# Block-sparse attention with a gated convolution: low words of w_out and of the taps in PSUM, ten more zero products, another order of all pieces

## The chip, the cores and the metric

The kernel runs on one core of one Trainium2 chip. The metric is device time in microseconds of one execution. The core's engines are named as in the profile: PE is TensorE, DVE VectorE, ACT ScalarE, POOL GpSimd, and SP the engine from whose queue every DMA is issued. Each engine works through its own list of instructions in order and waits where an instruction needs another engine's result.

## The reference

Four sequences of 768 positions, eight heads of 64. Each query sees the 31 keys around it and 24 summaries of blocks of 32 (maximum of the keys, mean of the values). The heads' outputs side by side are `x` (4 x 768 x 512), which goes through a causal convolution of five taps, a sigmoid gate and two 512 x 512 products:

```python
k_sum = k.reshape(B, H, nb, block, D).max(axis=3)
v_sum = v.reshape(B, H, nb, block, D).mean(axis=3)
scores_l = np.where(mask_l, scale * q @ k.T, -1e9)
scores_s = scale * q @ k_sum.T + np.log(block)
a = softmax(np.concatenate([scores_l, scores_s], axis=-1))
x = a @ np.concatenate([v, v_sum], axis=2)
gate_pre = sum(conv_w[k] * xp[:, k:k + S, :] for k in range(5))
out = (1 / (1 + np.exp(-gate_pre)) * (x @ w_val)) @ w_out
```

## The kernel before, in words

The work is cut into 24 units `u` (sequence, third of 256 positions, half of the heads) and 12 groups `g` (sequence, third; two units each). Everything is fp32. A product at full precision for the late groups is made of three cheaper ones: each factor is split into a rounded head (`xh`, `gh`, slot 0 of `wsplit`) and the rest (`xl`, `gl`, slot 1).

For a unit, `mm_s` puts the scores of two tiles into PSUM on TensorE (L558), `snorm` adds the mask and finds the minimum of the negated scores on VectorE (L573), `exps` is ScalarE's exponential (L586), `row_sum` and `recip` give 1/sum (VectorE), `norm` scales the rows (GpSimd, L600), `tp` transposes on TensorE (L610), `pcopy` brings the result to SBUF, `mm_x` multiplies by the values (L621, or L639 and L641 in the first and last units). `x_full`, `x_add`, `x_head` and `x_rest` make `xf`, `xh`, `xl`. `ginit` and `tap` (four per unit and half, VectorE, L677) are the convolution, `gate` a tanh. For a group, `val_mm` (L705) multiplies by `w_val`, `gated` (VectorE, L713) applies the gate, `out_mm` (L745) multiplies by `w_out`, and `out_scale` and `out_store` send the result away. Group 0 uses the unsplit weights `wf` in both products.

The weights arrive as 8-byte words. The high word of each is turned into a partial float by `rebias` on ScalarE (`sc`, L387). `low_bits` on VectorE shifts the low word right by 29 (L392), and `join` on VectorE puts both together (L396). `w_val` and `w_out` come in four pieces each (`wv0` to `wv3`, `wo0` to `wo3`, 128 x 512), the convolution's taps in one of 128 x 20 (`cw`, result `cwt`). In the kernel before, `low_bits` writes to the place in SBUF where the joined weight will stand, and `join` reads it there. `sc` of `w_val` lies in PSUM, that of the others in SBUF. PSUM has the pool `ps_p` with three banks, used by `val`, `out`, two small transposes and `sc` of `w_val`.

Nothing is scheduled by rules: `ORDER` (L54 to L138) is a list of 1265 words, one for each piece of work, and each engine receives the instructions of its pieces in that order. `W0` to `W23` (`warm_mm`, L335) are products of a tile of zeros, bf16, 512 columns, whose result nobody reads. In the word `ks0.1` the piece is `key_max` of sequence 0 and pair of heads 1 (VectorE, L258), `kc` copies its result into the key tile (GpSimd), `s0.0` is `mm_s` of unit 0, first half, `n0.1.0` `snorm` of unit 0, `Lk`, `Lq`, `Lv`, `Lu`, `Lwo` are loads of keys, queries, values, transposed values and raw weights, `F` fills the sums of the values into a loaded value tile (L369), `O` stores a result (L766), `rb`, `sh` and `or` with a weight's name are `rebias`, `low_bits` and `join`; `rbc`, `shc`, `orc` the same for the taps.

```python
    def join(dst, sc):
        d = dst.bitcast(U32)
        nc.vector.scalar_tensor_tensor(
            d, sc.bitcast(U32), 3, d, ALU.logical_shift_left, ALU.bitwise_or
        )
```

Of the kernel before, what the change touches and what calls it, by code (L numbers as in the profile page):

```python
# [60 lines left out]
m1.0 vt2.2 vc3.1 vc3.0 vt2.3 vt2.4 vc2.0 vc2.1 W23 s3.1 s3.0 t1.1 e2.0.1 e2.1.1 vbc0 rbwv0 shwv2
cd0.1 shwv0 n3.0.0 rr2 n3.0.1 orc rv2 n3.1.0 e3.0.0 c1.1 orwv0 orwv2 rbwv1 shwv1 orwv1 n3.1.1
x0.1 x0.0 t1.0 vb1 Lk1.0 Y0 I0.0 T0.0.0 T0.0.1 ks1.0 wcpwv0 m2.0 m2.1 wcpwv2 wlwv0 wlwv2 Lwv3
Lv1 v0.0.0.0 s4.1 s4.0 c1.0 vbc1 e3.1.1 I0.1 e3.0.1 e3.1.0 rbwv3 n4.0.1 n4.1.1 T0.0.2 n4.1.0
n4.0.0 v0.1.1.0 v0.0.1.0 t2.0 t2.1 c2.0 e4.0.1 c2.1 T0.0.3 rr3 rv3 T0.1.0 T0.1.1 T0.1.2 T0.1.3
e4.0.0 e4.1.0 Lu1.2 Lk1.1 Lq3 Lk1.3 F1 Lk1.2 s5.0 s5.1 x1.0 x1.1 n5.1.0 shwv3 n5.0.0 orwv3
n5.0.1 ks1.1 n5.1.1 G0 Y1 m3.1 kc1.0 m3.0 tv1.2 kc1.1 wcwv1 I1.0 v0.1.0.0 t3.0 I1.1 e4.1.1
T1.1.0 rr4 T1.0.0 rv4 T1.0.1 v0.1.1.1 v0.1.0.1 t3.1 c3.0 wcwv3 c3.1 s6.0 s6.1 x2.1 x3.0 x2.0
x3.1 v0.0.0.1 v0.0.1.1 Lv2 Lu1.1 Lwo0 Lq4 Lwo1 Lu1.0 F2 Lwo2 Lwo3 ks1.3 T1.1.1 n6.1.0 n6.0.1
T1.0.2 n6.0.0 ks1.2 T1.0.3 n6.1.1 T1.1.2 gf0.0 T1.1.3 wlwv1 wlwv3 m4.0 kc1.3 hal1 m4.1 kc1.2  # L70
e5.0.1 e5.1.1 X2 Y2 Y3 X3 Z2 Z3 e5.1.0 e5.0.0 e6.0.0 t4.0 t4.1 G1 I2.1 s7.0 s7.1 n7.0.0 n7.1.1
rr5 n7.0.1 n7.1.0 I2.0 T2.0.0 T2.1.0 rv5 T2.0.1 shwo0 T2.1.1 gf0.1 c4.0 e6.1.0 e7.0.1 e6.1.1
rbwo0 c4.1 e6.0.1 rbwo1 T2.1.2 T2.0.2 orwo0 T2.1.3 shwo1 rr6 T2.0.3 orwo1 shwo2 hal2 tv1.1 m5.0
m5.1 tv1.0 v1.1.0 v1.0.0 v1.0.1 v1.1.1 Lu1.3 Lu2.0 s8.1 x4.0 s8.0 x4.1 e7.0.0 Y4 rbwo2 rv6 G2
Ya4 orwo2 m6.0 o0.0.0 o0.0.1 t5.0 rbwo3 c5.0 I3.0 I3.1 shwo3 n8.1.1 orwo3 t5.1 o0.0.2 t6.0
o0.0.3 gf1.0 T3.1.0 n8.0.0 T3.0.0 tv1.3 c5.1 c6.0 e7.1.0 ob0.0 e7.1.1 Xp4 m6.1 Z4 wcpwo0 T3.1.1
n8.0.1 T3.0.1 rr7 T3.0.2 n8.1.0 T3.0.3 T3.1.2 rv7 T3.1.3 o0.1.0 o0.1.1 o0.1.2 vsp1 x5.1 x5.0
s9.0 s9.1 e8.0.1 e8.0.0 vsc1 tv2.0 wcpwo1 Y5 m7.0 Lv3 Ya5 Lk2.1 Lq5 Lu2.1 O0.0 Lk2.0 F3 Lq6
# [802 lines left out]
```

## Time and profile before

| what | us |
|---|---|
| three runs, median (lowest to highest) | 236.69 (235.08 to 236.76) |
| the profiled execution: its own time | 237.33 |
| its span, first to last instruction | 235.2 |
| TensorE busy | 224.5 |
| VectorE busy | 202.3 |
| GpSimd busy | 173.5 |
| ScalarE busy | 165.3 |

The span is what the trace shows; 2.13 us of the profiled execution's own time lie around it. This execution is 0.64 us above the median. Matmuls are recorded with modelled ends, and the products of scores, values and unsplit weights are recorded twice, so that 8 of them stand as x16.

### The profile page before, as it was taken

Reading aid. Unit: us, or ns where it says so; the run is one execution under the profiler, and the core shown is the slowest. Engines: PE = TensorE matmul, PEld = TensorE weight load, DVE = VectorE, ACT = ScalarE, POOL = GpSimd, SP = SyncE. Lnnn points to the kernel's source line nnn. Section 1 sums busy time; section 2 is a strip of 40 time slices with the busy share of each in tenths; the row PEclk is TensorE's granted clock in tenths of the full one; section 3 lists DMA queues with packets and bytes.
Section 4 is the critical chain, followed back from the end, with each engine's and each line's share of the span. In section 5 each row is a group of like instructions: output and inputs, shape, how many; then the busy total and the mean of one; then the engine's idle time right before and its main releaser. Section 6 shows DMA issues by size and latency. Waiting matters only on the chain.

```text
span 235.2 us, 8434 instructions
## 1 busy us (share of the span) xinstructions
PE 224.5 (95%) x3200; PEld 191.8 (82%) x3200; DVE 202.3 (86%) x740; ACT 165.3 (70%) x562; POOL 173.5 (74%) x262
## 2 busy tenths in 40 slices
PE   7688899998999999999999999999999999999994
...
PEclk9979999999999999999999999999999999999999
...
GB/s 252 403 415 414 413 229 345 308 207 285 332 183 352 124 337 101 292 366 150 243 100 11 0 280 216 91 303 237 96 11 0 25 262 109 47 3 92 0 88 135
DMA packets 16167, 46.20 MB, mean 196 GB/s; under 512 B 2272, under 2 KB 2528, under 8 KB 16128
## 3 DMA queue, kind: packets, MB, share of 16 engines
...
## 4 chain that ended last, share of the span: by engine, by line
PE 64%; DVE 18%; DMA 7%; ACT 5%; issue 2%; SPq 2%; POOL 1%; DVEq 0%; ACTq 0%; POOLq 0%
PE out L745 22%; PE val L705 20%; PE s L558 7%; PE pt L610 6%; PE x L621 6%; DVE g L677 5%; DMA v<-in_vw_dram 4%; DVE sn L573 4%; DVE wf L396 3%; ACT p L586 3%; DMA k<-in_kq_dram 2%; PE x L639 2%; DVE ks L258 1%; DVE wf L392 1%; DMA v<-vs 1%
## 5 line engine op out<-in xcount | busy, mean ns | idle before, releaser
L677 DVE SCALAR_TENSOR_TENSOR g<-xf,cwt,g 128x256 f32<-128x256 f32 x192 | 93.2, 486 | 7.1 <-ACT g L219 3.3
L586 ACT ACTIVATE p<-sn,nm 128x120 f32<-128x120 f32 x192 | 73.5, 387 | 12.5 <-DVE nm L573 10.5
L600 POOL TENSOR_TENSOR p<-p,ri 128x480 f32<-128x480 f32 x48 | 47.5, 1001 | 17.3 <-DVE ri L596 10.5
L705 PE MATMUL val<-xh,wv 128*128 128x256 f32 x352 | 50.0, 285 | 0.1
L573 DVE CUSTOM_DVE_ANT_0 sn<-s,mask 128x120 f32<-128x120 f32 x192 | 44.0, 275 | 3.6 <-PE s L558 3.0
L705 PEld LDWEIGHTS val<-xh,wv 128*128 128x128 f32 x352 | 44.2, 189 | 1.6 <-issue 0.6
L745 PE MATMUL out<-wo,gh 128*128 128x512 f32 (+1 forms) x184 | 45.4, 389 | 0.0
L745 PEld LDWEIGHTS out<-wo,gh 128*128 128x128 f32 x184 | 32.4, 188 | 6.6 <-issue 0.5
L586 ACT ACTIVATION_READ_ACCUMULATOR p<-sn,nm 128x1 f32 x192 | 36.7, 191 | 0.0
L613 ACT COPY pts<-pt 120x512 f32<-120x512 f32 x44 | 24.8, 583 | 15.7 <-PE pt L610 15.7
L721 POOL TENSOR_TENSOR gl<-gf,gh 128x512 fp32r<-128x512 f32 x22 | 28.3, 1293 | 8.6 <-ACT gh L718 8.3
L661 POOL TENSOR_TENSOR xl<-xf,xh 128x512 fp32r<-128x512 f32 x22 | 28.7, 1311 | 6.6 <-DVE xf L652 5.0
L286 POOL TENSOR_TENSOR vT<-vT 128x384 f32<-128x384 f32 (+3 forms) x44 | 25.5, 580 | 3.7 <-DMA vT<-in_vT_dram 1.1
L705 PE MATMUL val<-xl,wv 128*128 128x256 f32 x176 | 27.6, 279 | 0.0
L610 PE MATMUL pt<-ident,p 128*120 128x128 f32 x192 | 26.8, 276 | 0.1
L610 PEld LDWEIGHTS pt<-ident,p 128*120 128x120 f32 x192 | 22.3, 138 | 4.2 <-issue 1.7
L558 PE MATMUL s<-k,q 64*64 64x120 f32 x704 | 24.5, 270 | 0.6 <-DVE ri L596 0.6
L684 ACT ACTIVATE gt<-g 128x512 f32<-128x512 f32 x24 | 14.3, 596 | 14.8 <-DVE g L677 14.8
L745 PE MATMUL out<-wo,gl 128*128 128x512 f32 (+1 forms) x92 | 23.8, 381 | 0.0
L705 PEld LDWEIGHTS val<-xl,wv 128*128 128x128 f32 x176 | 23.6, 189 | 0.0
L558 PEld LDWEIGHTS s<-k,q 64*64 64x64 f32 x704 | 18.5, 135 | 4.8 <-issue 3.0
L745 PEld LDWEIGHTS out<-wo,gl 128*128 128x128 f32 x92 | 16.9, 188 | 3.4
...
## 6 DMA issues: line engine op xcount, KB each, us to landing
...
```

The lines of the kernel that those rows point to most:

```text
L286: nc.gpsimd.tensor_tensor(dst, src[:, :, :n], src[:, :, n : 2 * n], ALU.add)
L558: nc.tensor.matmul(sp(u)[64 * e : 64 * e + 64, h, c * KW : c * KW + KW], qs[64 * h : 64 * h + 64, i * QT : i * QT + QT], ktile[b, pr][64 * ...
L573: nc.vector.tensor_tensor_reduce(sn(u)[:, n, :], sp(u)[:, h, c * KW : c * KW + KW], mask[:, mv, :], -1.0 / math.sqrt(D), 3.0e38, ALU.add, ...
L586: nc.scalar.activation(pr_(u)[:, n, :], sn(u)[:, n, :], AF.Exp, bias=nm(u)[:, n : n + 1], scale=-1.0, accum_out=rs(u)[:, n, 0:1],)
L600: nc.gpsimd.tensor_tensor(pr_(u)[:, w], pr_(u)[:, w], st["ri", u][:, w].unsqueeze(2).broadcast_to([P, TPU, KW]), ALU.mult,)
L610: nc.tensor.transpose(pt[:KW, i, :], pr_(u)[:, TPU * r + i, :], ident)
L613: (eng or nc.scalar.copy)(pts(u)[:, TPU * r : TPU * r + TPU], st.pop(("pt", u, r))[:KW])
L661: nc.gpsimd.tensor_tensor(xl(g)[:, two(hp), :], xf(g)[:, two(hp), HALO:], xh(g)[:, two(hp), :].bitcast(F32), ALU.subtract,)
L677: nc.vector.scalar_tensor_tensor(gp(u)[:, r], xf(g)[:, pr, o : o + SG], cwt[:, pr, o : o + 1], gp(u)[:, r], ALU.mult, ALU.add,)
L705: nc.tensor.matmul(pp[:, r], w, x, start=first and n == 0, stop=last and n == len(terms) - 1)
L721: nc.gpsimd.tensor_tensor(gl(g)[:, two(cp), :], grp["gf", g, cp], gh(g)[:, two(cp), :].bitcast(F32), ALU.subtract)
L745: nc.tensor.matmul(pp, x, w, start=start and n == 0, stop=stop and n == len(terms) - 1)
```

## The change

`low_bits` of the four pieces of `w_out` and of the taps now writes to a tile of its own from `ps_p` in PSUM (`low_put`), and `join` reads the low word there. For `w_val` nothing is changed in this. `ORDER` has ten more zero products, `W24` to `W33`, all its other words stand in another order, and 55 of them name another engine for a copy, a scaling or a cast. Of the list only the beginning and one line are shown.

```diff
--- before.py
+++ after.py
@@ -52,89 +52,89 @@
-ez wz W0 W1 W2 W3 W4 Mi Mu W5 W6 W7 W8 W9 cv Lk0.0 Mm ks0.0 kc0.0 s0.0 W10 Lk0.1 Lk0.2 ks0.1
...
+ez wz W0 W1 W2 W3 W4 W5 Mu Lk0.0 Lk0.1 Mm ks0.0 ks0.1 kc0.0 W6 W7 W8 W9 W10 W11 W12 W13 W14 W15
+W16 W17 W18 W19 W20 W21 s0.0 W22 W23 W24 Lk0.3 Lk0.2 Lc Lwv0 Ln1 Ln0 Ln2 Lq1 Lwv1 Lv0 Lwv2 Ln3
...
@@ -391,15 +391,20 @@
         low = raw.rearrange("p (n two) -> p two n", two=2)[:, 0]
         eng.tensor_scalar(dst.bitcast(U32), low, 29, None, ALU.logical_shift_right)
 
-    def join(dst, sc):
-        d = dst.bitcast(U32)
+    def low_put(nm, n, raw):
+        t = ps_p.tile([P, DM], F32, tag="pp", name=f"low_{nm}")
+        lows[nm] = t[:, :n]
+        low_bits(nc.vector, lows[nm], raw)
+
+    def join(dst, sc, low):
         nc.vector.scalar_tensor_tensor(
-            d, sc.bitcast(U32), 3, d, ALU.logical_shift_left, ALU.bitwise_or
+            dst.bitcast(U32), sc.bitcast(U32), 3, low.bitcast(U32), ALU.logical_shift_left, ALU.bitwise_or
         )
 
     wide = wv.dtype != F32
     wraw = {}
     scaled = {}
+    lows = {}
     wf = cpool.tile([P, 4, DM], F32, tag="wf", name="wf")
 
     def load_w(nm, k):
@@ -416,12 +421,15 @@
 
     def w_low(nm, k):
         if wide:
-            low_bits(nc.vector, wf[:, k], wraw[nm, k])
+            if nm == "wo":
+                low_put(f"wo{k}", DM, wraw[nm, k])
+            else:
+                low_bits(nc.vector, wf[:, k], wraw[nm, k])
 
     def w_join(nm, k):
         raw = wraw.pop((nm, k))
         if wide:
-            join(wf[:, k], scaled.pop((nm, k)))
+            join(wf[:, k], scaled.pop((nm, k)), lows.pop(f"{nm}{k}", wf[:, k]))
         else:
             nc.vector.tensor_copy(wf[:, k], raw.bitcast(F32))
 
@@ -449,11 +457,11 @@
 
     def cw_low():
         if wide:
-            low_bits(nc.vector, cflat, wraw["cw"])
+            low_put("cw", NPR * NK, wraw["cw"])
 
     def cw_join():
         if wide:
-            join(cflat, scaled.pop("cw"))
+            join(cflat, scaled.pop("cw"), lows.pop("cw"))
 
     units = [(b, th, hp) for b in range(B) for th in range(NTH) for hp in range(NHP)]
     NG = B * NTH
```

On VectorE at the start of the program, while the first three units' scores are worked on (`sn_2` is unit 2, `cwt` the taps, `ks_0_2` the key maxima of sequence 0 and pair 2, `ri_0` the row sums of unit 0, `vpad` sums of values), before and then now:

```order
L613 COPY pts_0_313<-pt_0_0_269 120x512
L573 ISA sn_2_315,nm_2_316<-s_2_275,mask_99 128x120
L573 ISA nm_2_316 128x1
L573 ISA sn_2_315,nm_2_316<-s_2_275,mask_99 128x120
L573 ISA nm_2_316 128x1
L392 TENSOR_SCALAR cwt_101<-cwraw_197 128x20
```

```order
L392 TENSOR_SCALAR low_cw_251<-cwraw_177 128x20
L258 TENSOR_REDUCE ks_0_2_253<-k_0_2_175 128x24
L581 ISA sn_1_255,nm_1_256<-s_1_242,mask_99 128x120
L581 ISA nm_1_256 128x1
L581 ISA sn_1_255,nm_1_256<-s_1_242,mask_99 128x120
L581 ISA nm_1_256 128x1
L601 TENSOR_REDUCE ri_0_259<-rs0_109 128x8
L392 TENSOR_SCALAR wf_108<-raw_wv0_179 128x512
L604 RECIPROCAL ri_0_259<-ri_0_259 128x8
L309 TENSOR_REDUCE vpad_103<-vT_0_1_181 128x12
```

The shift of the taps' low words has moved from the middle of unit 2's scores to a place between units 0 and 1, and writes `low_cw` instead of `cwt`.

On VectorE where `w_out` is joined, some 50 us into the program (`g_2` is the convolution of unit 2, `xf_2` the attention's output of group 2, `gf_1_0` the gated product of group 1), with the waits of each instruction, before and then now:

```order
L392 TENSOR_SCALAR wf_108<-raw_wo0_745 128x512 [waits DMAHW0_49]
L677 SCALAR_TENSOR_TENSOR g_2_823<-xf_1_787,cwt_101,g_2_823 128x256 [waits DVE_49]
L713 SCALAR_TENSOR_TENSOR gf_0_1_861<-gt_0_638,val_0_1_527 128x512
L677 SCALAR_TENSOR_TENSOR g_2_823<-xf_1_787,cwt_101,g_2_823 128x256 [waits DVE_49] x2
L396 SCALAR_TENSOR_TENSOR wf_108<-sc_wo0_872,wf_108 128x512 [waits Activation_49]
L677 SCALAR_TENSOR_TENSOR g_2_823<-xf_1_787,cwt_101,g_2_823 128x256 [waits DVE_49]
L392 TENSOR_SCALAR wf_108<-raw_wo1_749 128x512 [waits DMAHW2_49]
L593 TENSOR_REDUCE ri_6_884<-rs2_111 128x8 [waits Activation_49]
L677 SCALAR_TENSOR_TENSOR g_2_823<-xf_1_787,cwt_101,g_2_823 128x256 [waits DVE_49]
L396 SCALAR_TENSOR_TENSOR wf_108<-sc_wo1_877,wf_108 128x512 [waits DVE_49,Activation_49]
L392 TENSOR_SCALAR wf_108<-raw_wo2_757 128x512 [waits DMAHW0_49]
L596 RECIPROCAL ri_6_884<-ri_6_884 128x8 [waits DVE_49]
L657 TENSOR_TENSOR xf_2_889<-xf_2_889,x_4_1_971 128x2x256 [waits PE_49,Activation_49]
L396 SCALAR_TENSOR_TENSOR wf_108<-sc_wo2_1013,wf_108 128x512 [waits DVE_49,Activation_49]
```

```order
L392 TENSOR_SCALAR low_wo0_930<-raw_wo0_726 128x512 [waits DMAHW0_49]
L685 SCALAR_TENSOR_TENSOR g_2_842<-xf_1_661,cwt_101,g_2_842 128x256 [waits DVE_49]
L400 SCALAR_TENSOR_TENSOR wf_108<-sc_wo0_862,low_wo0_930 128x512 [waits DVE_49,Activation_49]
L685 SCALAR_TENSOR_TENSOR g_2_842<-xf_1_661,cwt_101,g_2_842 128x256 [waits DVE_49]
L392 TENSOR_SCALAR low_wo2_994<-raw_wo2_728 128x512 [waits DMAHW1_49,DVE_49]
L685 SCALAR_TENSOR_TENSOR g_2_842<-xf_1_661,cwt_101,g_2_842 128x256 [waits DVE_49]
L400 SCALAR_TENSOR_TENSOR wf_108<-sc_wo2_969,low_wo2_994 128x512 [waits DVE_49,Activation_49]
L685 SCALAR_TENSOR_TENSOR g_2_842<-xf_1_661,cwt_101,g_2_842 128x256 [waits DVE_49]
L665 TENSOR_TENSOR xf_2_973<-xf_2_973,x_4_1_938 128x2x256 [waits PE_49,Activation_49]
L721 SCALAR_TENSOR_TENSOR gf_1_0_1016<-gt_1_1013,val_1_0_882 128x512 [waits Activation_49]
L392 TENSOR_SCALAR low_wo3_1043<-raw_wo3_1023 128x512 [waits DMAHW0_49,DVE_49]
L400 SCALAR_TENSOR_TENSOR wf_108<-sc_wo3_1039,low_wo3_1043 128x512 [waits DVE_49,Activation_49,Pool_49]
```

The shifts write `low_wo` tiles instead of `wf`, a shift and its join stand closer together, piece 1 comes earlier than the part shown, and the shifts of pieces 2 and 3 wait for VectorE's own earlier work.

In SP's queue of DMAs, where the values of group 8 are loaded and filled (`v_8`, and its four fills from `vs_2`), before and then now:

```order
L369 DMA v_6_2180<-vs_2_2101 12x2x512 x4
L249 DMA v_7_2274<-in_vw_dram 128x1024 x2
L369 DMA v_7_2274<-vs_2_2101 12x2x512 x4
L766 DMA out_0_dram<-ob_4_0_2593 128x512
L242 DMA vT_3_2_2596<-in_vT_dram 128x768
L230 DMA q_10_2598<-in_qT_dram 128x1024
L242 DMA vT_3_0_2600<-in_vT_dram 128x768
L249 DMA v_8_2636<-in_vw_dram 128x1024 x2
L766 DMA out_0_dram<-ob_3_1_2323 128x512
L369 DMA v_8_2636<-vs_2_2101 12x2x512 x4
```

```order
L369 DMA v_6_1910<-vs_2_2136 12x2x512 x4
L249 DMA v_7_2201<-in_vw_dram 128x1024 x2
L242 DMA vT_3_3_2342<-in_vT_dram 128x768
L774 DMA out_0_dram<-ob_1_0_1486 128x512
L369 DMA v_7_2201<-vs_2_2136 12x2x512 x4
L249 DMA v_8_2550<-in_vw_dram 128x1024 x2
L242 DMA vT_3_0_2553<-in_vT_dram 128x768
L774 DMA out_0_dram<-ob_4_0_2641 128x512
L230 DMA q_10_2646<-in_qT_dram 128x1024
L369 DMA v_8_2550<-vs_2_2136 12x2x512 x4
```

The load of `v_8` has moved ahead of a load of transposed values, a store and a load of queries, and one load of transposed values stands between it and the fills where there was a store.

## Rows read from the trace of the kernel before

**Rows 1.** The page: busy time by engine; TensorE's busy tenths and clock in 40 slices
```profile
PE 224.5 (95%) x3200; PEld 191.8 (82%) x3200; DVE 202.3 (86%) x740; ACT 165.3 (70%) x562; POOL 173.5 (74%) x262
...
PE   7688899998999999999999999999999999999994
...
PEclk9979999999999999999999999999999999999999
```

**Rows 2.** Busy time in stretches: from:to, length, busy us (xinstructions) by engine, PEclk, DMA
```profile
0.00:10.00 10.00, 7.45 (x49) 2.76 (x49) 5.64 (x19) 2.74 (x9) 3.51 (x19) 1.00 0.82 313
...
10.00:20.00 10.00, 7.20 (x96) 4.93 (x100) 9.08 (x53) 8.08 (x39) 6.77 (x17) 0.83 1.03 413
...
30.00:40.00 10.00, 10.00 (x217) 8.86 (x215) 9.86 (x44) 9.60 (x35) 8.65 (x14) 1.00 0.81 263
...
50.00:60.00 10.00, 9.10 (x121) 5.21 (x114) 10.00 (x25) 8.40 (x25) 9.07 (x12) 1.00 0.65 234
...
150.00:160.00 10.00, 9.60 (x163) 8.78 (x161) 9.17 (x32) 5.49 (x19) 9.75 (x12) 1.00 0.86 270
...
230.00:236.00 6.00, 2.10 (x18) 1.89 (x16) 0.00 (x0) 0.77 (x2) 0.00 (x0) 0.90 0.24 88
```

**Rows 3.** The chain that ended last: start us, us, what ran
```profile
57.26 3.70 PE out L745 x8
...
137.57 9.61 DMA v<-in_vw_dram
...
221.06 11.05 PE out L745 x60
...
232.13 0.38 ACT ob L219
```

**Rows 4.** Timeline of TensorE (PE) and its weight loads (PEld), first 20 us
```profile
1.52 4.45 PE L335 MATMUL warm_out<-warm 128*128 128x512 bf16 x10 [1.52 <-POOL warm L330]
...
4.91 0.15 PEld L335 LDWEIGHTS <-warm 128*128 128x128 bf16 x1 [0.28 <-issue]
...
6.22 0.64 PE L558 MATMUL s<-k 64*64 64x120 f32 x16 [0.25 <-POOL k L272]
...
13.14 1.08 PE L558 MATMUL s<-k 64*64 64x120 f32 x16 [1.13 <-POOL k L272]
```

**Rows 5.** Timeline of VectorE (DVE), first 20 us; idle time and its releaser in brackets
```profile
8.22 0.28 DVE L573 CUSTOM_DVE_ANT_0 sn<-s,mask 128x120 f32<-128x120 f32 x1 [1.27 <-PE s L558]
...
11.87 0.17 DVE L593 TENSOR_REDUCE ri<-rs 128x8 f32<-128x16 f32 x1 [0.22 <-ACT p L586]
...
14.28 0.28 DVE L573 CUSTOM_DVE_ANT_0 sn<-s,mask 128x120 f32<-128x120 f32 x1 [0.31 <-PE s L558]
...
17.05 0.28 DVE L573 CUSTOM_DVE_ANT_0 sn<-s,mask 128x120 f32<-128x120 f32 x1 [0.36 <-PE s L558]
```

**Rows 6.** Lines 396 and 392: count, duration ns min/median/max, first and last start
```profile
L396 DVE SCALAR_TENSOR_TENSOR wf<-sc_wv,wf x4: 673/680/691, 23.2 to 34.0; 128x512 uint32<-128x512 uint32 x4
L396 DVE SCALAR_TENSOR_TENSOR wf<-sc_wo,wf x4: 759/1134/1491, 49.5 to 56.1; 128x512 uint32<-128x512 uint32 x4
L396 DVE SCALAR_TENSOR_TENSOR cwt<-sc_cw,cwt x1: 960/960/960, 21.8 to 21.8; 128x20 uint32<-128x20 uint32 x1
...
L392 DVE TENSOR_SCALAR wf<-raw_wo x4: 419/435/826, 47.3 to 55.0; 128x512 uint32<-128x512 uint32 x4
L392 DVE TENSOR_SCALAR cwt<-cwraw x1: 756/756/756, 17.5 to 17.5; 128x20 uint32<-128x20 uint32 x1
```

**Rows 7.** Timeline of GpSimd (POOL), 53 to 66 us
```profile
54.46 1.07 POOL L648 CAST xh<-xf 128x512 fp32r<-128x512 f32 x1
...
64.13 0.61 POOL L648 CAST xh<-xf 128x512 fp32r<-128x512 f32 x1
```

**Rows 8.** Timeline of TensorE, 52 to 61 us
```profile
52.97 1.13 PE L745 MATMUL out<-wf,gf 128*128 128x512 f32 x2 [0.17 <-ACT sc_wo L387]
...
57.26 3.70 PE L745 MATMUL out<-wf,gf 128*128 128x512 f32 x8 [0.57 <-DVE wf L396]
```

More of the change, by code (lines that the diff above doesn't have):

```diff
@@ L61 @@
[L61 to L78, printed above, removed]
@@ new lines @@
+T0.1.0 rv2 T0.1.1 ks1.0 e3.0.0 e3.1.0 I0.0 e3.1.1 e3.0.1 c1.1 vt3.0 vt3.1 vt3.2 vt3.3 vt3.4
+vc3.0 vt2.3 vt2.4 vc2.1 m2.1 vc3.1 vc2.0 m2.0 kc1.0 Lq2 s4.1 s4.0 Lwv3 Lv1 Lk1.2 Lk1.1 T0.1.2
+n4.0.0 n4.1.0 n4.0.1 T0.0.0 n4.1.1 T0.0.1 shwv3 rr3 v0.0.1.0 v0.1.1.0 vb1 t2.1 e4.1.0 vbc1 s5.1
+s5.0 T0.1.3 rv3 n5.1.0 T0.0.2 n5.0.0 T0.0.3 e4.0.0 e4.1.1 c2.1 rbwv3 x1.0 x1.1 Lk1.3 G0 Y1
+wcpwv2 I1.1 n5.1.1 orwv3 ks1.2 T1.1.0 n5.0.1 ks1.1 v0.0.0.0 t2.0 c2.0 e4.0.1 m3.1 wcpwv1 m3.0
+wlwv1 wlwv2 kc1.1 hal1 wcpwv3 wlwv3 kc1.2 v0.1.1.1 I1.0 v0.1.0.1 v0.0.1.1 t3.1 t3.0 e5.0.0
@@ new lines @@
+T6.0.1 T6.1.3 T6.0.2 rv9 ks2.2 x8.0 s12.0 Y8 e11.1.0 m9.0 hal4 m9.1 Z6 kc2.2 n12.0.0 T6.0.3 G6
+Ya8 I7.0 ob2.1 I7.1 rr10 ks2.3 n12.1.0 n12.0.1 n12.1.1 T7.1.0 T7.0.0 rv10 rr11 T7.0.1 T7.1.1
+T7.1.2 rv11 T7.1.3 o2.0 t9.0 t9.1 c9.1 c9.0 v3.1.1 kc2.3 x9.1 s13.0 s13.1 x9.0 e12.1.1 Lv5 Lq7
+Lu2.1 Lk3.1 Lk3.3 F5 e12.0.0 e12.1.0 Y9 tv2.1 v3.1.0 v3.0.0 n13.1.1 T7.0.2 T7.0.3 G7 I8.1 I8.0
+n13.0.0 n13.0.1 Ya9 n13.1.0 m10.1 m10.0 X9 m11.1 Lu2.2 tv2.2 Xp8 Z8 Z9 t10.1 t10.0 v3.0.1
+e12.0.1 c10.1 e13.1.1 gf3.1 T8.0.0 cd10.0 T8.0.1 rr12 T8.1.0 rv12 T8.0.2 T8.0.3 T8.1.1 T8.1.2
```

133 lines of the change are left out of this document (69 added, 64 removed).

## The prediction

> **What bounds the kernel now.** I read the page first, then the busy time in stretches, the chain that ended last, and the timelines of the places that these point to. On the page TensorE is busy 224.5 of 235.2 us, and its row of tenths is full from the sixth slice to the last but one [rows 1]. The stretches say it more sharply (the engines stand in the order PE, PEld, DVE, ACT, POOL): TensorE is busy 7.45 and 7.20 us of the first two tens, all 10.00 in 30 to 40, 9.10 in 50 to 60, 9.60 in 150 to 160, and 2.10 of the last six [rows 2]. The chain ends with 11.05 us of TensorE's products and a 0.38 us copy from 232.13 on [rows 3]. So the end is set by the start-up, in which TensorE has little to do, then by TensorE's own work, with idle time of 0.9 and 0.4 us in two of the later stretches, and by a tail of about 3 us (2.10 of 6 busy, then copy and store). Products are neither removed nor made shorter. The change can only move the start-up, these small gaps, and make new ones.
>
> The start-up is VectorE's. Its first score piece begins at 8.22, after 1.27 us of waiting for scores, and three short waits follow (0.22, 0.31, 0.36 us) [rows 5]; over 10 to 20 it is busy 9.08, over 50 to 60 all 10.00 [rows 2]. The last two of the three waits are for score products that ran slowly: 16 records took 0.64 us at 6.22 and 1.08 us at 13.14 [rows 4], in the stretch whose granted clock is 0.83, so partly at 1.2 GHz and not at 2.4 [rows 2].
>
> **The change, part by part.** I add up against the profiled execution's own 237.33 us, which lies 0.64 above the median of the three runs, and take that off at the end.
>
> *Zero products ahead of the first scores.* Before, ten stand there and take 4.45 us from 1.52 on; the weights of the tenth are loaded at 4.91 [rows 4], so they follow each other at (4.91 - 1.52) / 8 = 0.42 us, which is the lower clock, since the scores behind them already ran at the short time. Now 22 stand ahead of `s0.0` (the list's first words in the diff). If the clock rises when it did, the first ten end near 5.9 and the twelve others take half as long each, 12 x 0.21 = 2.5 us: `s0.0` starts near 8.4 and ends 0.64 later, and VectorE's first score piece starts near 9.1 instead of 8.22. Before, it began with the second half of the scores, now with the first, so not the whole shift of 2.2 us arrives. Cost +0.9 us on VectorE, bounds 0 and +3.9 (a rival below). The other twelve zero products (34 in all, 22 ahead) stand in TensorE's waits for the next scores; I take them at nothing, and 0.2 us each where such a wait is gone.
>
> *The three short waits.* The next scores now come when VectorE still has key maxima, the taps' shift and a piece of `w_val` to do. I take all 0.9 us as gone, bounds 0 and -0.9.
>
> *The taps.* Their shift took 0.756 us and their join 0.960 for 20 columns, while a join of 512 columns of `w_val` took 0.680 [rows 6]. So it isn't the columns that cost: another small piece on this engine takes 0.17 [rows 5]. What sets the two apart from `w_val`'s join is that both their tensors lie in SBUF, with GpSimd at work beside them. With the low word in PSUM I take 0.2 us each: -1.3 us, bounds 0 and -1.4. Both stand on the path, as VectorE is the engine that the start-up waits for.
>
> *The clock in the start-up.* Zero products keep TensorE at work until near 11 us. Then, as before, it waits for VectorE piece by piece, and the clock may fall again, now between 14 and 22 us, where five groups of 16 score records and the first values' product stand. Each group then costs 0.44 more (1.08 - 0.64), 2.2 us in all, part of it beside VectorE's other work. I take +0.7, bounds 0 and +2.2. The start-up sums to +0.9 - 0.9 - 1.3 + 0.7 = -0.6.
>
> *The four pieces of `w_out`.* Their joins took 1.134 us in the median, up to 1.491, against 0.680 for those of `w_val`, whose high part lies in PSUM [rows 6]. With one tensor in PSUM I take 0.68: 4 x 0.45 = 1.8 us less on VectorE. GpSimd gains too: a cast took 1.07 us beside these joins and 0.61 at 64 us [rows 7]. But only what TensorE waited is on the path: it was idle 0.9 us in this stretch [rows 2], of which the rows name 0.17 for ScalarE's part of `w_out` and 0.57 for the last join [rows 8]. I take -0.9, bounds -1.2 and +0.9. The upper end is the added wait: a low word needs one of three banks, and of `wo3` it holds the one that the second output tile of group 0 needs. Behind that tile's first product stand the rest of group 0's output, the values of unit 5 and the scores of unit 9. The product that follows needs `wo3`'s join in any case, so late joining costs one product here, no more than 1.13 us for two records [rows 8].
> The row has the shift of `w_out`'s low words at 0.435 us, and I leave it at that. The Trainium skill (VectorE: DVE Perf Modes, "Why PSUM operands drop a tier") says that an fp32 operand in PSUM holds an instruction to one element per cycle. An estimate from that page's 0.96 GHz is 512 / 0.96 = 0.53 us, so 0.4 us more for four; by it this part would be -0.5 and the forecast 0.4 later. No row here has a shift into PSUM.
>
> *The new order from 60 us on.* The load of group 8's values took 9.61 us from 137.57 [rows 3], and TensorE lost 0.4 us in 150 to 160, after it. SP's queue now has that load ahead of a store, of queries and of transposed values, so it should land earlier; I take half, -0.2. What new gaps the order makes can't be read from rows of the old one: I take 0, bounds -0.4 and +2.5 (as much as the whole start-up lost in its first ten us, 10.00 - 7.45). The tail keeps its pieces: last product of half a tile, copy, store.
>
> Sum: -0.6 - 0.9 - 0.2 = -1.7. 237.33 - 1.7 = 235.6, less 0.64 is **235.0 us**.
>
> **The rivals.**
> *More is gained.* The clock holds through the start-up (+0.7 falls away), and GpSimd's saved time lets scales and casts come earlier, so that both later gaps vanish (-0.2 - 0.3). For it: more zero products exactly where the clock fell, and the slow casts of rows 7. Against it: zero products end near 11 us, and the slow stretch of before began at 13. Time 235.0 - 1.2 = 233.8, or less.
> *The order pays it back.* TensorE is full from 30 us on, so each piece that is late by more than its slack shows, and 1275 words in a new order have many chances. For it: VectorE is busy 86%, and gaps of 0.9 and 0.4 exist even now. Against it: TensorE's row of tenths shows no slice below 8 after the first third of the program, except the last [rows 1]. With +1.9 of new gaps: 236.9.
> *Slower: the zero products overrun.* They stand in TensorE's queue ahead of the first scores, and if they all run at the lower clock, 22 end at 1.6 + 22 x 0.42 = 10.9, the first scores at 12.0 instead of 6.9; VectorE starts 3.9 late, and the next nine products cost 0.21 more each, 1.9. With the taps and `w_out` still gained: 237.33 + 3.9 + 1.9 - 1.3 - 0.9 - 0.64 = 240.3. For it: the first ten all ran slowly. Against it: the scores right behind them did not. It decides from the eighth product on that runs slowly after the tenth (8 x 0.21 = 1.7 eats the forecast).
>
> **How the numbers follow.** Forecast 0.50, more gained 0.20, paid back 0.20, overrun 0.10. About 1% (2.4 us) is what a measurement of this kernel can tell from no change. Faster by more than that is below 234.3: the second case and a fifth of the forecast's, 0.30. Slower is above 239.1: the overrun, and a fifth of the paid-back case, 0.14. Within, 0.56. The range leaves out most of the overrun, and the outer part of the second case: 232.6 to 239.0. Below, the sum of all lower bounds (-1.4 - 0.9 at the start, -1.2, -0.4) is -3.9, so 232.8; above, the forecast with the bound of +2.5 for new gaps and the clock's full cost is 235.0 + 2.5 + 1.5 = 239.0.
>
> **What would show it right or wrong.** Right: VectorE's first score piece near 9.1 us; the taps' two pieces near 0.2 us; the joins of `w_out` near 0.68 and TensorE's busy time in 50 to 60 near 10; TensorE full from about 28 us; the last product about 1.7 us before 232.1. Wrong in the start: zero products still 0.42 us apart after the tenth, or granted clock below 0.83 in 10 to 20 and low in 20 to 30. Wrong in the rest: stretches after 60 us in which TensorE's busy time is below 9.6, and a chain that there runs through VectorE, GpSimd or a load of values.

## The result, and the profile after

The changed kernel took 233.86 us in the median of six executions (233.49 to 234.50), the kernel before 236.72 (235.08 to 237.78) in six beside it: ratio 0.9887, 95% interval 0.9851 to 0.9923. That is 2.9 us faster, where the forecast of 235.0 expected 1.7. It lies in the range, and at the time of the case "more is gained" (233.8). How large the gain is depends on the executions of before that it is set against, since these are a mixture (shown further below): in a later series, in which that kernel's median was 235.57, the changed kernel was 1.8 us faster (233.78), at a ratio of 0.9908. The profiled execution took 233.49, its span is 231.7 us.

The page of the changed kernel, against [rows 1]: the same engines, VectorE 2.6 us less busy, TensorE's tenths full from the fifth slice to the last but one, and no slice of its clock below 9.

```profile
PE 224.4 (97%) x3210; PEld 191.9 (83%) x3210; DVE 199.7 (86%) x743; ACT 165.4 (71%) x564; POOL 169.0 (73%) x257
...
PE   7988999999999999999999999999999999999994
...
PEclk9999999999999999999999999999999999999999
```

Busy time in stretches, in the columns of [rows 2]:

```profile
0.00:10.00 10.00, 8.37 (x46) 3.33 (x47) 4.22 (x18) 2.02 (x5) 2.64 (x18) 1.00 0.80 298
10.00:20.00 10.00, 8.29 (x131) 5.11 (x135) 9.99 (x56) 9.60 (x44) 8.12 (x17) 1.00 1.03 414
50.00:60.00 10.00, 10.00 (x147) 5.84 (x136) 9.23 (x38) 9.99 (x37) 8.93 (x15) 1.00 0.99 362
150.00:160.00 10.00, 10.00 (x133) 9.26 (x133) 8.27 (x31) 5.36 (x11) 6.41 (x8) 1.00 0.20 48
200.00:210.00 10.00, 9.71 (x118) 8.54 (x116) 8.98 (x18) 5.13 (x10) 4.30 (x5) 1.00 0.01 2
```

The clock stays at 1.00 from 10 to 20 us (0.83 before). VectorE is busy 9.99 there, where it had been busy 9.08. TensorE's idle 0.90 in 50 to 60 and 0.40 in 150 to 160 are gone; 0.29 is new in 200 to 210. In the chain, the last products begin at 217.46, where before they began at 221.06 [rows 3]:

```profile
217.46 11.05 PE out L753 x60
```

So TensorE ends 3.6 us earlier. The later stretches account for 0.9 + 0.4 - 0.2 = 1.1 of that (TensorE was busy 9.92 in 200 to 210 before), which leaves 2.5 for the first 30 us (its idle time there fell from 6.2 to 3.8). The timeline of TensorE there, against [rows 4]:

```profile
1.53 6.77 PE L335 MATMUL warm_out<-warm 128*128 128x512 bf16 x22 [1.53 <-POOL warm L330]
...
13.09 0.64 PE L566 MATMUL s<-k 64*64 64x120 f32 x16 [0.33 <-POOL k L272]
```

The 22 zero products begin 0.42 us apart; from the eleventh weight load on they take half of that (12 loads in 2.47 us):

```profile
5.33 2.47 PEld L335 LDWEIGHTS <-warm 128*128 128x128 bf16 x12 [0.27 <-issue]
```

The scores that took 1.08 us at 13.14 now take 0.64 at 13.09. VectorE's timeline, against [rows 5]:

```profile
8.94 0.28 DVE L581 CUSTOM_DVE_ANT_0 sn<-s,mask 128x120 f32<-128x120 f32 x1 [2.23 <-PE s L566]
...
11.46 0.18 DVE L392 TENSOR_SCALAR low_cw<-cwraw 128x20 uint32<-128x20 uint32 x1
11.54 0.94 DVE L258 TENSOR_REDUCE ks<-k 128x24 f32<-128x768 f32 x1
...
17.20 0.17 DVE L400 SCALAR_TENSOR_TENSOR cwt<-sc_cw,low_cw 128x20 uint32<-128x20 uint32 x1
17.32 0.20 DVE L604 RECIPROCAL ri<-ri 128x8 f32<-128x8 f32 x1
```

The first score piece is at 8.94 after 2.23 us of waiting, and the three short waits that followed it do not come back. The taps' shift takes 0.18 us and their join 0.17, and the instructions behind them begin 0.08 and 0.12 us after them. In the kernel before it was 0.67 and 0.88:

```profile
17.47 0.76 DVE L392 TENSOR_SCALAR cwt<-cwraw 128x20 uint32<-128x20 uint32 x1
18.14 0.27 DVE L573 CUSTOM_DVE_ANT_0 sn<-s,mask 128x120 f32<-128x120 f32 x1
...
21.85 0.96 DVE L396 SCALAR_TENSOR_TENSOR cwt<-sc_cw,cwt 128x20 uint32<-128x20 uint32 x1
22.73 0.19 DVE L596 RECIPROCAL ri<-ri 128x8 f32<-128x8 f32 x1
```

So the taps hold VectorE up by 0.20 us instead of 1.55. The joins and shifts of `w_out`, against [rows 6] (duration ns min/median/max):

```profile
L400 DVE SCALAR_TENSOR_TENSOR wf<-sc_wo,low_wo x4: 676/680/687, 43.3 to 53.2; 128x512 uint32<-128x512 uint32 x4
```

```profile
L392 DVE TENSOR_SCALAR low_wo<-raw_wo x4: 683/686/694, 40.6 to 52.3; 128x512 uint32<-128x512 uint32 x4
```

The joins fell from 1.134 to 0.680 us, as forecast. The shifts rose from a median of 0.435 (mean 0.53, one took 0.826) to 0.686, which was not in the forecast.

### The profile page after: what moved, and what is told of

It reads as the page before. It is cut to its first block, busy times and chain, and to the rows that moved or that the text cites. A ratio compares the mean times of both kernels' runs of the same rounds, so it can differ in the third digit from the quotient of the medians.

```text
span 231.7 us, 8482 instructions
## 1 busy us (share of the span) xinstructions
PE 224.4 (97%) x3210; PEld 191.9 (83%) x3210; DVE 199.7 (86%) x743; ACT 165.4 (71%) x564; POOL 169.0 (73%) x257
## 4 chain that ended last, share of the span: by engine, by line
PE 83%; DVE 11%; ACT 3%; issue 1%; POOL 0%; ACTq 0%; DVEq 0%; POOLq 0%
PE out L753 28%; PE val L713 25%; PE s L566 8%; PE pt L618 8%; PE x L629 7%; DVE g L685 4%; PE warm_out L335 3%; DVE sn L581 2%; PE x L647 2%; DVE wf L400 1%; DVE vpad L309 1%; ACT gt L692 1%; DVE ks L258 1%; PE vsp L355 1%; DVE gf L721 1%
## 5 line engine op out<-in xcount | busy, mean ns | idle before, releaser
L608 POOL TENSOR_TENSOR p<-p,ri 128x480 f32<-128x480 f32 x48 | 46.7, 987 | 14.6 <-DVE ri L604 11.6
L669 POOL TENSOR_TENSOR xl<-xf,xh 128x512 fp32r<-128x512 f32 x22 | 28.2, 1287 | 12.6 <-ACT xh L656 6.9
L621 ACT COPY pts<-pt 120x512 f32<-120x512 f32 x42 | 23.6, 578 | 10.1 <-PE pt L618 10.1
L286 POOL TENSOR_TENSOR vT<-vT 128x384 f32<-128x384 f32 (+3 forms) x44 | 25.0, 569 | 2.9 <-DMA vT<-in_vT_dram 0.3
L618 PEld LDWEIGHTS pt<-ident,p 128*120 128x120 f32 x192 | 21.7, 137 | 5.1 <-POOL p L608 2.2
L566 PE MATMUL s<-k,q 64*64 64x120 f32 x704 | 23.3, 267 | 0.3 <-DVE g L685 0.3
L219 ACT ACTIVATE ob<-out 128x512 f32<-128x512 f32 (+1 forms) x21 | 11.9, 574 | 11.2 <-PE out L753 7.2
```

The costliest lines, as they stand in the source:

```text
L286: nc.gpsimd.tensor_tensor(dst, src[:, :, :n], src[:, :, n : 2 * n], ALU.add)
L566: nc.tensor.matmul(sp(u)[64 * e : 64 * e + 64, h, c * KW : c * KW + KW], qs[64 * h : 64 * h + 64, i * QT : i * QT + QT], ktile[b, pr][64 * ...
L608: nc.gpsimd.tensor_tensor(pr_(u)[:, w], pr_(u)[:, w], st["ri", u][:, w].unsqueeze(2).broadcast_to([P, TPU, KW]), ALU.mult,)
L618: nc.tensor.transpose(pt[:KW, i, :], pr_(u)[:, TPU * r + i, :], ident)
L621: (eng or nc.scalar.copy)(pts(u)[:, TPU * r : TPU * r + TPU], st.pop(("pt", u, r))[:KW])
L669: nc.gpsimd.tensor_tensor(xl(g)[:, two(hp), :], xf(g)[:, two(hp), HALO:], xh(g)[:, two(hp), :].bitcast(F32), ALU.subtract,)
```

## The experiments

Ratios are against runs of the kernel before on the same chip. One mark serves for comparing start-ups: the time at which TensorE begins the first product of `wo` with `gh` (the output of group 1, split weights). It is comparable between kernels of the same order only; in the kernel before it is 73.08.

### The place of the low words, and the order

The changed kernel with the low words in SBUF, in two series:

```diff
-            if nm == "wo":
+            if nm == "none":
...
-            low_put("cw", NPR * NK, wraw["cw"])
+            low_bits(nc.vector, cflat, wraw["cw"])
...
-            join(cflat, scaled.pop("cw"), lows.pop("cw"))
+            join(cflat, scaled.pop("cw"), cflat)
```

> The changed kernel, its order and its 34 zero products, with the low words of the taps and of w_out written to SBUF as before. Theory (PSUM gave most of the gain): the taps' two pieces cost VectorE some 1.3 us more in the start-up, the four joins of w_out 0.45 each more and their shifts 0.25 each less, 0.8; about 1.9 of the 2.9 us come back, ratio to the kernel before near 0.996, TensorE idle by 0.5 or more in 50 to 60 us. Rival (the order gave it, the place of the low words nothing): ratio stays at 0.988 to 0.990, with joins above 1.0 us and no idle TensorE in 50 to 60. Rival (only the start counts): taps' pieces near 0.8 us, ratio near 0.994, TensorE full in 50 to 60.

> The changed kernel with all low words in SBUF, once more, now on one chip with the changed kernel. Theory (the place of the low words is worth next to nothing in the new order: VectorE's shift of the taps delayed the next instruction by 0.08 us in either place, and TensorE was full in 50 to 60): within 0.3 us of the changed kernel, ratio 0.988 to 0.992. Rival (it is worth what the first trace's span says, 233.0 against 231.7): 1 us or more behind the changed kernel, ratio 0.993 or above.

Beside the second series, the changed kernel itself, once more:

> The changed kernel unchanged, once more, as the measure for the three runs beside it. Expected ratio 0.988 to 0.991. Where the 22 zero products end is expected to differ from one execution to the next: in three traces so far with 22 ahead of the first scores they took 6.77, 7.22 and 7.53 us; the first score group begins between 8.2 and 9.0.

Measured: 234.10 us, ratio 0.9909 (0.9874 to 0.9943), and 234.58, ratio 0.9911 (0.9877 to 0.9944); the changed kernel beside the second 233.78, ratio 0.9908 (0.9873 to 0.9943). Over both series the low words in SBUF stand at 234.41 (17 executions), the changed kernel over three series at 233.84 (22 executions). None of the sizes forecast holds: by the medians the place is worth about 0.6 us (0.4 by the means), far less than 1.9. That it is more than nothing is likely, not shown: the ratios of the two kernels in one series overlap, and resampling all executions gives -0.1 to 0.9 for the difference of the medians. Where it may sit is seen in two traces whose first scores begin alike. The changed kernel, in its third series:

```profile
8.91 0.64 PE L566 MATMUL s<-k 64*64 64x120 f32 x16
...
72.69 1.65 PE L753 MATMUL out<-wo,gh 128*128 128x512 f32 x6
```

The one with low words in SBUF, in its second series:

```profile
8.95 0.64 PE L566 MATMUL s<-k 64*64 64x120 f32 x16
...
73.20 1.20 PE L753 MATMUL out<-wo,gh 128*128 128x512 f32 x4
```

From a start 0.04 us apart the mark is 0.51 apart. TensorE has no idle time in 50 to 60 either way (the first trace with low words in SBUF has a wait of 0.48 us just ahead of it, at 49.55, for a transfer that fills values):

```profile
50.00:60.00 10.00, 10.00 (x181) 6.32 (x174) 9.65 (x37) 9.56 (x33) 9.38 (x15) 1.00 0.95 349
```

And VectorE's timeline in the same trace shows why the taps give little in this order:

```profile
12.18 0.72 DVE L392 TENSOR_SCALAR cwt<-cwraw 128x20 uint32<-128x20 uint32 x1
12.26 0.94 DVE L258 TENSOR_REDUCE ks<-k 128x24 f32<-128x768 f32 x1
...
17.92 0.30 DVE L400 SCALAR_TENSOR_TENSOR cwt<-sc_cw,cwt 128x20 uint32<-128x20 uint32 x1
18.15 0.19 DVE L604 RECIPROCAL ri<-ri 128x8 f32<-128x8 f32 x1
```

The shift is recorded with 0.72 us, but the next instruction begins 0.08 later and takes what it always takes. The join of 0.30 holds the next up by 0.23, where in PSUM it is 0.12. So in the new order PSUM is worth 0.11 us for the taps.

The rest comes in later: group by group, the two traces of TensorE drift apart by 0.2 us at 49 and by another 0.36 between 58.8 and 65 us. Around there VectorE's eight pieces for `w_out` take 6.0 us in all with low words in SBUF and 5.5 in PSUM. The larger price stands on GpSimd: its three like groups of sums (L286) between 43 and 57 us take 2.96, 3.34 and 3.01 us beside the joins in SBUF, and 2.52, 2.50 and 2.49 with low words in PSUM. By 60 us it is 1.17 us late with its scaling (60.63 against 59.46), and the transposes at 61.67 begin when this scaling ends (60.63 + 0.99). So the rest of the 0.6 goes to `w_out`, in good part by way of GpSimd. That is read from these traces, not shown by a run of its own.

The other side, the order and the zero products of before with low words in PSUM:

```diff
-n2.0.0 shc n2.1.0
+n2.0.0 n2.1.0
...
-orc rv2
+shc orc rv2
...
-c5.0 I3.0 I3.1 shwo3
+c5.0 I3.0 gf1.0 shwo3
...
-gf1.0 T3.1.0
+I3.1 T3.1.0
```

> The order and the zero products of before, with the low words in PSUM. Two words of the order are moved, since the banks would run out otherwise: the taps' shift stands right ahead of their join, and one gated piece of group 1 changes places with a start of the convolution ahead of the shift of wo3. Theory (PSUM gave most of the gain): taps' pieces near 0.2 us, joins of w_out near 0.68, TensorE idle by less than 0.3 us in 50 to 60 us (0.9 before); ratio near 0.992. Rival (the order gave it): pieces as short, but the time falls into other waits; ratio 0.998 to 1.002.

Measured: 244.64 us, ratio 1.0361 (1.0326 to 1.0396), the opposite of both. The granted clock was low as well in all six executions (means of 0.972 to 0.986), but most of the 8 us is this: TensorE stood still.

```profile
50.77 2.08 PE L709 MATMUL val<-xh,wv 128*128 128x256 f32 x8 [6.56 <-DVE wf L396]
```

VectorE's timeline beside it:

```profile
47.54 0.69 DVE L388 TENSOR_SCALAR low_wo<-raw_wo 128x512 uint32<-128x512 uint32 x1
...
50.04 0.68 DVE L396 SCALAR_TENSOR_TENSOR wf<-sc_wo,low_wo 128x512 uint32<-128x512 uint32 x1
...
60.55 0.69 DVE L661 TENSOR_TENSOR xf<-xf,x 128x512 f32<-128x512 f32 x1 [7.08 <-ACT xf L656]
```

The values product of group 1 waited 6.56 us and was released when the first join of `w_out` had read its low word (50.04 + 0.68), so for one of the three banks, as it reads nothing that this join writes. TensorE had been ready for it from 44.21 on, 3.3 us before VectorE came to write that low word. In the order of before the shift and the join of `wo0` are 2.5 us apart, with convolution steps and a gated piece between them, just where that product needs the bank; in the new order one tap stands between them, and TensorE waits for no bank in this stretch. Behind the late values product came the attention products for `xf`, for which VectorE waited 7.08 us with the two last joins queued behind. The low words of `w_out` in PSUM need the new order, or one like it.

The taps alone in PSUM, in the order of before:

```diff
-n2.0.0 shc n2.1.0
+n2.0.0 n2.1.0
...
-orc rv2
+shc orc rv2
```

> The kernel before with the taps' low word alone in PSUM, its shift moved to stand right ahead of its join. In the trace of before the two pieces held up VectorE's next instruction by 0.67 and 0.88 us. Theory (both stand on the path of the start-up): the pieces hold up VectorE by 0.2 us together, group 1's output products begin near 71.8 instead of 73.08, ratio 0.994 to 0.996. Rival (beside TensorE's slow clock and the loads they cost next to nothing): pieces as short, group 1's output products between 72.7 and 73.3, ratio 0.998 to 1.002.

Measured: 234.91 us, ratio 0.9947 (0.9919 to 0.9975), at first sight the first theory. But the trace shows another thing as well. TensorE, with the mark in the last row:

```profile
11.22 0.64 PE L562 MATMUL s<-k 64*64 64x120 f32 x16 [1.49 <-DVE nm L577]
...
13.31 0.64 PE L562 MATMUL s<-k 64*64 64x120 f32 x16 [1.13 <-POOL k L268]
...
15.04 1.05 PE L562 MATMUL s<-k,q 64*64 64x120 f32 x32 [0.29 <-issue]
...
71.11 2.09 PE L749 MATMUL out<-wo,gh 128*128 128x512 f32 x8
```

The two waits of 1.49 and 1.13 us are those of before, yet the transposes take 0.65 and the scores 1.05 at 15.04, and the clock did not fall:

```profile
10.00:20.00 10.00, 7.02 (x119) 4.88 (x119) 9.75 (x57) 9.14 (x45) 8.11 (x20) 1.00 1.03 415
```

So 71.11 against 73.08 is not the taps' doing alone. Against a trace of the old order in which the clock held too (71.46, next part) it is 0.35 us, though unit 1's first scores began 0.33 later than there (11.22 against 10.89), so 0.68 from an equal start. The times say the same: the eight executions of this run in which the clock held have a median of 234.73, those of the kernel before in which it held 235.57 (45; the seven on this chip 236.13), and the kernel before with ten more zero products 235.50 (12). So in the old order the taps' low word in PSUM is worth some 0.8 us. The pieces hold VectorE up by 0.29 us together, where 0.2 was expected.

The place alone does not make the shift slow. With ten more zero products it writes to SBUF as before and yet takes 0.17 us, beside a short copy on GpSimd (16.37 to 16.83). The 0.756 and 0.794 us of the two traces of before stood beside GpSimd's sums (L318).

### The zero products and the clock

The kernel before with ten more zero products in the two waits:

```diff
 W16
+W24 W25 W26 W27 W28 W29
 s1.0 W17
+W30 W31 W32 W33
 kc0.3 rr0 rv0
```

> The kernel before with ten more zero products: six behind the sixth of those ahead of s1.0, four ahead of s1.1. In its trace TensorE waited 1.49 and 1.13 us there, and the granted clock is 0.50 from 13 to 16 us. Theory (the clock's fall costs on the path): clock 1.00 from 10 to 20, the score group of 1.08 us becomes 0.64, the second of 1.36 becomes 1.05, first work after it earlier by 0.5 to 1.3 us; ratio 0.995 to 0.998. Rival (VectorE sets the start-up, TensorE's slow products lie beside its work): clock 1.00, ratio 0.999 to 1.001. Rival (zero products in the way): scores later, ratio above 1.001.

Measured: 235.50 us, ratio 0.9979 (0.9956 to 1.0002). The clock holds, and the mark is 1.6 us earlier than in the trace of before (0.16 of it stood there already at unit 1's first scores, 10.89 against 11.05):

```profile
10.00:20.00 10.00, 8.74 (x128) 5.49 (x126) 9.75 (x60) 9.14 (x45) 8.23 (x20) 1.00 1.03 412
```

```profile
71.46 2.09 PE L741 MATMUL out<-wo,gh 128*128 128x512 f32 x8
```

The gain in time is smaller than in this trace, since the time of before is a mixture, as the last run shows:

> The kernel before, unchanged, against itself. Its times fall into two groups, near 235.4 and from 236.3 up. Its one trace so far is of an execution of 237.33 us in which the granted clock was 0.50 from 13 to 16 us; with only the taps' low word moved, a trace shows the same two waits of 1.49 and 1.13 us, no fall of the clock, and 234.75 us. Theory (the same waits let the clock fall in some executions and not in others, and this makes the two groups): either clock 1.00 in 10 to 20, group 1's output products near 71.7 us and a time of at most 235.7, or the fall again, those products near 73.1 and a time from 236.2 up. Rival (the groups come from something else): a clock of 1.00 with a time from 236.2 up, or a fall with at most 235.7. Ratio 0.997 to 1.003 in any case.

Measured: 236.72 us, ratio 1.0003 (0.9973 to 1.0033); the profiled execution took 236.72, and its trace is that of before again:

```profile
11.10 0.64 PE L558 MATMUL s<-k 64*64 64x120 f32 x16 [1.49 <-DVE nm L573]
...
13.77 1.00 PE L610 MATMUL pt<-ident,p 128*120 128x128 f32 x4
...
15.12 1.88 PE L558 MATMUL s<-k,q 64*64 64x120 f32 x32
...
73.15 1.17 PE L745 MATMUL out<-wo,gh 128*128 128x512 f32 x4
```

```profile
15.00:16.00 1.00, 1.00 (x21) 0.88 (x23) 1.00 (x3) 1.00 (x7) 0.92 (x2) 0.50 1.05 430
```

The same two waits, then 1.00 us for four transposes, 1.88 for 32 score records, and the mark at 73.15. Each execution's mean granted clock is known. Of 89 executions of the kernel before in the series beside the experiments, 44 had a mean of at most 0.993 and took 236.43 to 238.46, median 236.76. The other 45 had 0.998 or more and took 234.97 to 237.59, median 235.57; 36 of them are faster than any of the first. So the fall comes in half of the executions, and those with it are 1.2 us longer. With the ten zero products none of the twelve executions had a mean below 0.998, and their median of 235.50 is that of the executions without the fall.

The changed kernel without the twelve zero products behind the first scores:

```diff
-s0.0 W22 W23 W24
+s0.0
...
-W25 s0.1 W26 W27 W28 W29 W30
+s0.1
...
-W31 s1.0 W32
+s1.0
...
-W33 c0.1
+c0.1
```

> The changed kernel without the twelve zero products that stand behind s0.0; the 22 ahead of it stay. Theory (the clock is held by those in the waits): TensorE idles some 1 us twice between 9 and 13 us, the granted clock falls to 0.50 for some 3 us between 11 and 17; scores and transposes take up to 1.08 instead of 0.64; 0.7 to 1.3 us later, ratio 0.992 to 0.994. Rival (VectorE sets the start-up whatever the clock): clock falls, ratio stays at 0.988 to 0.990. Rival (22 ahead are enough): clock 1.00 throughout, ratio 0.988 to 0.990.

Measured: 235.48 us, ratio 0.9969 (0.9947 to 0.9991): 1.6 behind the changed kernel. That is the first theory's outcome, with more than its 0.7 to 1.3 us: the clock stayed low for 7 us, where 3 were forecast. All twelve executions had a mean clock of 0.983 to 0.985. The trace:

```profile
13.57 1.08 PE L562 MATMUL s<-k 64*64 64x120 f32 x16 [0.65 <-POOL k L268]
...
17.16 1.88 PE L562 MATMUL s<-k,q 64*64 64x120 f32 x32
...
21.95 0.34 PE L643 MATMUL x<-pts,v 120*64 120x64 f32 x4
```

```profile
10.00:20.00 10.00, 7.18 (x94) 5.55 (x95) 8.94 (x51) 8.36 (x39) 7.31 (x16) 0.66 1.04 413
```

TensorE had waited 1.07, 1.25 and 0.65 us before each of three score groups; then comes the slow stretch (1.08 for 16 records, 1.88 for 32; the granted clock is 0.50 to 0.56 from 13 to 20), and the first attention products of unit 0 stand at 21.95. In the changed kernel it is 20.30, from first scores that began 0.45 earlier.

### Twenty-two ahead, and the loads

The changed kernel with 12 zero products ahead of the first scores, alone and with a load moved:

```diff
-W12 W13 W14 W15 W16 W17 W18 W19 W20 W21 s0.0
+s0.0
```

> The changed kernel with 12 zero products ahead of the first scores instead of 22, 24 in all as in the kernel before, the twelve in the waits as in the changed kernel. Theory (the ten more ahead only delay VectorE; the clock is held by those in the waits): the first score group begins near 6.5 us, VectorE's first score piece near 7.2 instead of 8.9, clock 1.00 from 10 to 20; 0.8 to 1.7 us faster than the changed kernel, ratio 0.982 to 0.986. Rival (the clock needs the 22): granted clock of 0.50 somewhere between 7 and 20 us, ratio 0.990 or above. Rival (the earlier start meets other waits, keys and weights still on their way): clock held, VectorE idle for 1 us or more between 8 and 20, ratio as the changed kernel's within 0.002.

Measured: 233.88 us, ratio 0.9884 (0.9832 to 0.9936), the time of the third outcome, but not its sign: VectorE was not idle between 8 and 20. It began 1.5 us earlier, and TensorE then waited for queries at 24.30. The two timelines:

```profile
7.39 0.28 DVE L577 CUSTOM_DVE_ANT_0 sn<-s,mask 128x120 f32<-128x120 f32 x1 [0.44 <-PE s L562]
```

```profile
24.30 1.05 PE L562 MATMUL s<-k,q 64*64 64x120 f32 x32 [1.05 <-DMA q<-in_qT_dram]
```

The load of these queries was issued behind a load of keys that waits for its buffer. Moved ahead of it:

```diff
-Lk1.0
+Lq2 Lk1.0
...
-kc1.0 Lq2 s4.1
+kc1.0 s4.1
```

> The changed kernel with 12 zero products ahead of the first scores and, in addition, the load of group 2's queries issued ahead of the load of sequence 1's first keys. With 12 ahead alone, VectorE began 1.5 us earlier and the time stayed; TensorE then waited 1.05 us for these queries at 24.30. Their load stood in the queue behind a load of keys that waits for its buffer until 15.7 us. Theory (that wait alone takes the gain away): wait gone, output products of group 1 begin near 71.0 instead of 72.1, 0.7 to 1.2 us faster than the changed kernel, ratio 0.983 to 0.986. Rival (the start-up is bound by all transfers together, which run at their full rate from 10 to 30 us): another load is late by as much, keys or values, ratio 0.988 to 0.990.

> The changed kernel unchanged, as the measure for the runs beside it: ratio 0.988 to 0.991.

Measured: 233.05 us, ratio 0.9863 (0.9829 to 0.9897), beside 233.80, ratio 0.9882 (0.9859 to 0.9906), for the changed kernel. The wait is gone and the mark at 71.45 (71.94 with 12 ahead alone):

```profile
71.45 2.11 PE L749 MATMUL out<-wo,gh 128*128 128x512 f32 x8
```

It is the fastest median of all kernels here, but the intervals overlap: 0.7 us faster than the changed kernel is likely, not shown.

Last, the load of group 8's values, the third of the edits to the kernel before:

```diff
-Lu3.2 Lq10 Lu3.0 x14.1 x14.0 Lv8
+Lv8 Lu3.2 Lq10 Lu3.0 x14.1 x14.0
```

> The kernel before with the ten more zero products in its waits and, in addition, the load of group 8's values issued ahead of two loads of transposed values and one of queries instead of behind them. Without that second edit TensorE reached its output products of group 1 at 71.46 instead of 73.08 us, 1.6 earlier, but the span was only 0.8 shorter, and the wait for group 8's values 1.2 us instead of 0.4. Theory (that load gives half of the start-up's gain back): wait at most 0.3 us, span near 233.0, ratio near 0.993. Rival (something else later takes it): wait gone, span 234 or more, ratio 0.997 to 0.999. Rival (the load is set by the transfers, not by its place in the queue): wait still near 1.2.

Measured: 240.06 us, ratio 1.0157 (1.0103 to 1.0212). The wait for the values is gone, and a longer one has come. GpSimd, then TensorE:

```profile
145.71 2.51 POOL L282 TENSOR_TENSOR vT<-vT 128x384 f32<-128x384 f32 x4 [5.14 <-DMA vT<-in_vT_dram]
...
151.21 0.99 POOL L596 TENSOR_TENSOR p<-p,ri 128x480 f32<-128x480 f32 x1
```

```profile
152.25 1.11 PE L606 MATMUL pt<-ident,p 128*120 128x128 f32 x4 [3.09 <-POOL p L596]
```

The transposed values, now behind 1 MB of values, kept GpSimd waiting for 5.14 us. It sums them in its own order of work, and the scaling that TensorE needed stood behind these sums. None of the theories had this. And the wait that this edit removes is no fixed one: it is 0.40 us in the first trace of before, 1.21 with the ten zero products, and none in the second trace of before.

## Why the prediction was right, and where its sizes were off

The direction and the bound were right: nothing was taken from the products, TensorE ended earlier by what it no longer waited. What came is the case "more is gained", to which I gave 0.20: the clock held through the start-up, and both later gaps vanished. That the time also came out at its 233.8 is in part luck, since that sum took the clock at nothing and the other terms too high.

Medians divide the 2.9 us: from 236.72 to 235.57 by the clock (the executions of before in which it held), from there to 234.41 by the order (low words in SBUF), from there to 233.84 by the low words. That is 1.15, 1.16 and 0.57, over series on several chips, so each is good to some tenths, and the division is one of several: what the taps cost can be taken away by the order or by PSUM, and here the order comes first. Term by term:

- *Zero products ahead, +0.9.* The place was right (first score piece forecast at 9.1, measured 8.94). The cost can't be seen: with 12 ahead VectorE began at 7.39 and nothing was gained, since the queries of group 2 came too late, and with these loaded earlier a gain of 0.7 is likely, not shown. What failed is that 0.9 of the shift would arrive: as long as that load ends last, none of it does. The rival "they overrun" did not come: products speeded up from 5.33 on, in the middle of the 22 (in other traces up to 1.6 us later, with first scores at 8.99 at the latest).
- *Three short waits, -0.9.* They are gone. What they brought is part of the 1.15 and 1.16 and was not measured alone.
- *The taps, -1.3.* The pieces are as short as forecast, and VectorE is held up by 1.35 us less. Where the forecast went wrong is in giving all of it to PSUM and in taking it all as time of the kernel. In the old order PSUM alone brings some 0.8 us. In the new order with the low word still in SBUF the pieces hold VectorE up by 0.08 and 0.23, so most of the hold-up went by where they stand, and PSUM brings 0.11.
- *The clock, +0.7.* The wrong sign. I priced a fall that might come back and forgot that the time of before already paid for one. The row of the clock [rows 2] and the score group of 1.08 us [rows 4] had it: the profiled execution was one of those with the fall. Twelve zero products in the waits hold it off, and leaving them out costs 1.6.
- *`w_out`, -0.9.* The idle time of 50 to 60 is gone as forecast, but not by the place of the low words: it is gone with SBUF too, by the order. PSUM adds up to 0.5 on top, and, as the prediction had it, GpSimd gains: 1.8 us over its three groups of sums beside the joins. The upper bound of +0.9 for a bank held: in the new order TensorE waits for no bank. In the old order a bank held too long costs most of 8 us, so the low words in PSUM need an order like the new one to stay within that bound.
- *The shift into PSUM.* I left it at 0.435 us, and it took 0.686. The Trainium skill (VectorE: DVE Perf Modes, "Why PSUM operands drop a tier") has the direction right: an fp32 operand in PSUM caps the instruction at one element per cycle. The estimate of 0.53 us worked out from it counted the columns alone and is too low: from 20 columns to 512 the shifts into PSUM go from 0.176 to 0.686 us, so 1.04 ns a column, as that estimate has it, and 0.155 us come on top. By the means, the joins gained 0.45 us each and the shifts lost 0.16, so VectorE gained 0.29 us per piece, not 0.45. That a join of two tensors in SBUF is the slow one agrees with the same Trainium skill (SBUF — State Buffer, "SBUF: two separate sides"), by which a VectorE instruction with two inputs there and a GpSimd instruction that reads there exclude each other for a whole instruction: in the second trace with low words in SBUF the joins of `w_out` took 0.69 to 1.31 us, in the changed kernel 0.676 to 0.687.
- *After 60 us, -0.2.* The wait for group 8's values is gone, one new gap of 0.29 came. With a wait that is between 0 and 0.4 us in two traces of one kernel, a term of this size can't be told. The rival "the order pays it back" had its chance here, and found 0.29 of its 1.9.

So the sum of -1.7 was short by 1.2 us. The clock's term was off by 1.85 (+0.7 against -1.15), and the five others, -2.4 together, brought 1.73 (1.16 and 0.57), so 0.67 less than forecast. That the waits of TensorE make the clock fall is shown (waits filled, waits emptied), and so are the 1.2 us that go with it. How the 1.73 divides is argued, since no run has one stretch's order alone: the gap of 50 to 60 (0.9) and the taps (0.8 by PSUM in the old order) would fill it.

## What to carry to other kernels

Look at the granted clock in the stretch before pricing a wait there: an execution in which it fell carries a loss that filling the wait gives back, and the kernel's times may be a mixture of executions with and without it. Read what an instruction costs from the start of the next one on its engine, not from its own duration. A tile that is put into a small pool can hold up whoever needs the bank next until its last reader has run, and that can be longer than the tile is in use: 6.56 us here, with 3.2 from the start of the write to the end of the read. So the order has to be changed with it.

## What the runs showed of the chip

The fall of the clock is not a property of the kernel alone: in the kernel before the waits of 1.49 and 1.14 us led to a granted clock of 0.50, and in the run with the taps' low word moved the same waits, 1.49 and 1.13, did not. A row that says 1.00 doesn't yet mean that products run at 2.4 GHz: the first zero products followed each other at 0.42 us, which is the lower level, with a granted clock of 1.00 beside them. In the traces with the same 22 they speeded up between 5.3 and 6.95 us, and the first scores began between 8.19 and 8.99. What decides this stays open. In the trace without zero products in the waits, TensorE also stood still for 1.96 us at 70.28, in the middle of a values' product, for nothing that the profile shows; that too stays open.
